# A Fourier mixing layer fused with an ELU feed-forward: a PSUM tile of its own for one product, two copies moved to another engine, a weight sum cut in pieces

## The chip, the cores and the metric

The kernel runs on one core of a Trainium2 chip. The core has TensorE (matmuls, called PE in the profile, its weight loads PEld), VectorE (DVE), ScalarE (ACT), GpSimd (POOL) and SyncE (SP), which work side by side and wait for each other by semaphores. TensorE writes its results into PSUM, which has eight banks of 2 KB per partition; VectorE and ScalarE read them from there, and POOL works here on SBUF alone. The metric is the device time of one execution in microseconds, lower is better; the time before is the median of three runs.

## The reference

The input x has 8 batches of 3008 rows and 256 columns. Cut to what matters:

```python
X = np.fft.rfft(x, axis=1)
Xr, Xi = X.real, X.imag
Yr = Xr @ w_r - Xi @ w_i + b_r
Yi = Xr @ w_i + Xi @ w_r + b_i
Yr = sign(Yr) * maximum(abs(Yr) - 0.01, 0)          # the same for Yi
y = np.fft.irfft(Yr + 1j * Yi, n=3008, axis=1)      # 24064 x 256 over all batches
h = y @ w_in                                        # w_in 256 x 2048
g = where(h > 0, h, exp(minimum(h, 0)) - 1)         # ELU
out = g @ w_out                                     # w_out 2048 x 256, float32
```

## The kernel before

Each batch goes through a Fourier part in small units, and then through the feed-forward. The feed-forward sets the rhythm: it is one long run of 376 steps, 47 for each batch. Step i computes two 128-row slices of h for 512 rows of y (`front`, line 966: four bf16 matmuls of 512 columns, L986), the ELU of them (`elu` and `finish_elu`), and two steps later the part of the output that they give (`back`, line 1044: eight float32r matmuls of 256 columns, L1060). Every eighth step ends a block of 512 rows, and its output is copied from PSUM into `osb` (L1072), half by VectorE and half by ScalarE.

The units of the Fourier part of the next batch are put into the steps, at most one per step, by `plan` (line 1090): X (second stage of the forward transform, 8 units), M (the complex product with w_r and w_i, 12 units), B and Y (the inverse transform, 6 and 8 units) and A (first stage of the forward transform for the batch after, 6 units). In a middle batch the order is y2, y3, X0 to X7, M(0,0), M(0,1), y4, M(1,0), M(1,1), y5, B0, M(2,0), M(2,1), y6, B1, M(3,0), M(3,1), y7, B2, M(4,0), M(4,1), B3, M(5,0), M(5,1), A0, B4, B5, A1 and so on; the steps after that hold no unit.

The order of all instructions is that of the program (`manual_schedule`): each engine takes its own in the order in which they are written. In one step that is: the unit (its matmuls, and the copy of its result out of PSUM), the step's front matmuls, ScalarE's part of the ELU, then `finish_elu`, VectorE's last part of the ELU **of the step before** (gT, L1028 or L1030), then what stands in the list f1 (loads, other side work), then `elu`, and `back` of two steps ago.

The ELU has two forms that matter here. In a "pool" step ScalarE makes two exponentials of 512 columns (L1002), POOL takes the minimum with 1 (L1039), and VectorE makes gT in two pieces. In an "act" step ScalarE makes a relu and an exponential of 1024 columns (L1004, L1005), POOL has no part, and VectorE makes gT in one piece of 1024. Steps with an M unit are act steps, and so are those listed in `on_act` (line 1115): X4, X7, B3, A0 and y4 to y7. In those listed steps the unit's result is copied by VectorE; in the other X, Y, B and A units of a middle batch it is copied by ScalarE.

PSUM is shared out so: two banks for the output (`psO`), two slots of two banks for h (`psH`), and one slot of two banks (`psF`) for the units; in some free steps h goes there too (`third`). With two slots for h, the front matmuls of step i wait until VectorE has made gT of step i - 2. Every unit that takes the psF slot waits until the unit before it has been copied out.

From batch 2 on, M forms the complex product out of three real ones (`unit_M`, line 246). The sums Xr + Xi are made ahead by POOL (`sum_XT`, L206), and wcat_s is changed once into the differences of weights that this needs (`three_weights`, line 214, L218, two POOL operations). M's six matmuls (L269) write one psF tile: first the shared product, of the sum and w_r, into the second bank; then the other two products into the first. In the first unit, M(0,0), the shared product comes last, because its sum is the last to be ready. VectorE copies the shared product to SBUF (the copy of 256 columns, called from L275, at L126) and adds it to the other two (L276); POOL adds the bias and makes the soft threshold (L281 to L283), in three operations per M.

Copies out of PSUM go through the helper `evac`, so that they all stand at L126 (VectorE) or L128 (ScalarE); what is copied is told by the names of the tiles (XT<-xps for X, yT<-yps for Y, yb<-mps for M).

Of the kernel before, what the change touches and what calls it, by code (L numbers as in the profile page):

```python
# [11 lines left out]
F32 = mybir.dt.float32  # L12
# [17 lines left out]
def kernel(  # L30
# [12 lines left out]
    P = nc.NUM_PARTITIONS  # L43

    B, S, D = x.shape
# [15 lines left out]
    wcat_r = constp.tile([P, 2, 2 * D], BF16, name="wcat_r")  # L61
    wcat_s = constp.tile([P, 2, 2 * D], BF16, name="wcat_s")
# [14 lines left out]
    space = constp.tile([P, 384], BF16, name="space")  # L77
# [41 lines left out]
    def unit_ps(name, alone):  # L119
        if alone:  # L120
            return pre2.tile([P, 2, 512], F32, name=name, tag="pre2")
        return psF.tile([P, 2, 512], F32, name=name, tag="fps")

    def evac(dst, src, on_dve):
        if on_dve:
            nc.vector.tensor_copy(dst, src)  # L126
        else:
            nc.scalar.copy(dst, src)  # L128
# [82 lines left out]

        return XS[:, 3 * dt + ch] if 3 * dt + ch < 5 else busy[:]

    def three_weights(c):

        v, r = (w[:, :, D * c : D * c + D] for w in (wcat_s, wcat_r))
        a, b_ = (r, v) if c else (v, r)
        nc.gpsimd.tensor_tensor(v, a, b_, ALU.subtract)  # L218

# [26 lines left out]
    def unit_M(b, q, i):  # L246
        if b == 1:
            if i == 0:
                mps_of[q] = unit_ps("mps", False)
            yb, clip = m_group(b, q, i, mps_of[q][:, i, :])  # L250
            nc.gpsimd.tensor_scalar(clip[:], yb, LAM, -LAM, ALU.min, ALU.max)
            nc.gpsimd.tensor_tensor(Y_of[b, q][:, i, :], yb, clip[:], ALU.subtract)
            return
        XT, o = XT_of[b], (2 * q + i) * P
        if i == 0:
            Y_of[b, q] = wk3.tile([P, 2, 2 * D], BF16, name="Y", tag="Y")
        ps = unit_ps("mps", False)
        ch, oc = divmod(o, 512)
        r, s = wcat_r, wcat_s
        todo = [  # L260
            (ps[:, 1, 0:D], None, r[:, :, 0:D]),
            (ps[:, 0, 0:D], XT[:, :, 1, o : o + P], s[:, :, 0:D]),
            (ps[:, 0, D : 2 * D], XT[:, :, 0, o : o + P], s[:, :, D : 2 * D]),
        ]
        if o == 0:
            todo.append(todo.pop(0))
        for out_, lhs, w in todo:
            for dt in range(2):
                nc.tensor.matmul(  # L269
                    out_, lhsT=lhs[:, dt] if lhs is not None else sum_of(dt, ch)[:, oc : oc + P],  # L270
                    rhs=w[:, dt, :], start=(dt == 0), stop=(dt == 1),
                )
        yb = wk3.tile([P, 2 * D], F32, name="yb", tag="yb")
        clip = wk2.tile([P, 2 * D], F32, name="clip", tag="clip")
        evac(yb[:, D : 2 * D], ps[:, 1, 0:D], True)  # L275
        nc.vector.tensor_tensor(  # L276
            yb[:].rearrange("p (c d) -> p c d", c=2),
            ps[:, 0].rearrange("p (c d) -> p c d", c=2),
            yb[:, D : 2 * D].unsqueeze(1).to_broadcast([P, 2, D]), ALU.add,
        )  # L280
        nc.gpsimd.tensor_tensor(yb[:], yb[:], bias_bc[:], ALU.add)  # L281
        nc.gpsimd.tensor_scalar(clip[:], yb[:], LAM, -LAM, ALU.min, ALU.max)  # L282
        nc.gpsimd.tensor_tensor(Y_of[b, q][:, i, :], yb[:], clip[:], ALU.subtract)  # L283
# [682 lines left out]
    def front(i, third, on_act, halves):  # L966
        blk, fp = divmod(i, NPAIR)
        early = i < FILL
        if early:
            hps = two_banks((psS0, psS1)[i % 2], "sps")  # L970
        elif third:
            hps = psF.tile([P, 2, TB], F32, name="hps", tag="fps")
        else:
            hps = psH.tile([P, 2, TB], F32, name="hps", tag="hps")
        todo = []
        for s in range(2):
            ft = 2 * fp + s
            for piece in sorted(pieces(blk * TB, TB), key=lambda z: z[3] - z[2]):
                todo.append((s, ft, piece))
        if i == PER // NPAIR * NPAIR:  # L980
            todo.sort(key=lambda z: z[2][0])
        Et = late3.tile([P, 2, TB], F32, name="Et", tag="Et")
        E_ = Et[:]
        for s, ft, (b, t0, c0, c1) in todo:
            for dt in range(2):
                nc.tensor.matmul(  # L986
                    hps[s][:, c0:c1] if early else hps[:, s, c0:c1],
                    lhsT=w_in_s[:, dt, ft * P : ft * P + P],
                    rhs=yT_of[b][:, dt, t0 : t0 + c1 - c0],
                    start=(dt == 0), stop=(dt == 1),  # L990
                )
            if early and (dt, c1) == (1, TB):
                nc.scalar.activation(E_[:, s], hps[s][:], AF.Exp)
        if early:
            return hps, Et
        if i == n - 1:
            for h in range(2):
                t = slice(TB // 2 * h, TB // 2 * h + TB // 2)
                nc.scalar.activation(E_[:, :, t], hps[:, :, t], AF.Exp)
        elif halves:  # L1000
            for s in range(2):
                nc.scalar.activation(E_[:, s], hps[:, s], AF.Exp)  # L1002
        elif on_act:
            nc.scalar.activation(E_, hps[:], AF.Relu, scale=-1.0)  # L1004
            nc.scalar.activation(E_, E_, AF.Exp, scale=-1.0)  # L1005
        else:
            nc.scalar.activation(E_, hps[:], AF.Exp)
        return hps, Et
# [25 lines left out]
    def elu(i, hps, Et, on_pool, on_act):  # L1034

        E_ = Et[:]
        if on_pool:
            for s in parts(i):
                nc.gpsimd.tensor_scalar(E_[s], E_[s], 1.0, 0.0, ALU.min, ALU.max)  # L1039
        elif not on_act:  # L1040
            nc.vector.tensor_scalar(E_, E_, 1.0, -1.0, ALU.min, ALU.add)
        late_elu.append((i, hps, Et, on_pool or on_act, on_pool))
# [44 lines left out]
    def put(kind, b, *a):  # L1087
        return ({"A": unit_A, "X": unit_X, "M": unit_M, "B": unit_B, "Y": unit_Y}[kind], (b, *a))

    def plan(b):  # L1090
# [35 lines left out]
        for t, u in enumerate(seq, lead):  # L1126
            if b and n1 < B:
                mode[t] = "act" if u in on_act or u[0] == "M" else "pool"
            if mode[t] == "act" and u[0] != "M":
                k = {"y": "Y"}.get(u[0], u[0])  # L1130
                c = {"y": b, "A": n2}.get(u[0], n1)
                if c < B:
                    f0[t].append(put(k, c, u[1], False, *((False, True) if k == "B" else (True,))))
            elif u[0] == "y":
                f0[t].append(put("Y", b, u[1]))
            elif u[0] == "n":
                f0[t].append(put("Y", n1, u[1]))
            elif u[0] == "A":
                if n2 < B:
                    f0[t].append(put("A", n2, u[1]))  # L1140
            else:
                f0[t].append(put(u[0], n1, *u[1:]))
            if u == (("A", 1) if b and n2 < B else ("B", 5)):
                f1[t] += [
                    (load_Bs, (n1, w, 0, 4 * K1 - 16 * (b == w == 0))) for w in range(4)
                ]
            if u == ("A", 5) and n2 < B:
                f1[t] += [(load_Z, (n2, s0, s1)) for s0, s1 in ((0, 8), (8, NS))]
# [12 lines left out]
        if n2 < B:  # L1161
            for ci in range(3):
                f1[xs[ci]].append((load_x, (n2, ci)))
        if b == 1:
            for c in range(2):
                f1[2 * c].append((three_weights, (c,)))
        if b and n1 < B:
            for dt, t in ((0, 6), (1, 9)):
                f0[t].append((sum_XT, (n1, dt)))
# [5 lines left out]
    for i in range(n + LAG):  # L1175
        if i == FILL:
            few.close()
            psH, psF = (
                ctx.enter_context(
                    tc.tile_pool(  # L1180
                        name=n_, bufs=k_, space=bass.MemoryType.PSUM, reuse_waits="tile"
                    )
                )
                for n_, k_ in (("psH", 2), ("psF", 1))
            )
        if i == LAG:
            back(0, False)
# [21 lines left out]
        if i < n:  # L1209
            for f, a in f1[r]:  # L1210
                f(*a)
            split = i > LAG and (i - LAG) % NPAIR == NPAIR - 1
            if split:
                back(i - LAG, True)
            elu(i, *h, pooled, on_act)
            if 1 <= i < 5:
                if i < 3:
                    scale_w_in(2, True, i - 1)
                scale_w_in(3, False, (i - 1) // 2, (i - 1) % 2)
            if i == n - 2:  # L1220
                early_h = front(n - 1, True, False, True)
            elif early_h:
                early_h = None
        else:
            split = False
# [32 lines left out]
```

## Time and profile before

| | |
|---|---|
| median of 3 runs | 906.11 us (904.94 to 3122.65) |
| the profiled execution | 905.32 us, span 903.5 us |
| granted TensorE clock in it | 0.998 |
| DVE copy yb<-mps, 128x256 (L126) | 72 times, 424 ns |
| DVE sum yb<-mps,yb, 128x512 (L276) | 72 times, 691 ns |
| POOL L281, L282, L283 | 72 times each, 1280, 614 and 1284 ns |
| XT<-xps, 128x768, by ACT / by DVE | 47 times 798 ns / 13 times 958 ns |
| POOL sum of weights (L218) | 2 times, at 162.1 and 166.4 us, about 1165 ns |

One execution was recorded by the profiler; its span is the time between the first and the last instruction. A line of a timeline gives start and duration in microseconds, the engine, the line of the kernel, the operation, what it writes and reads, and, in square brackets, how long the engine had been idle just before and which engine's work ended that. A line of the list of waits reads: engine, what and line, "<-" what it waited for, then the total in microseconds, how often, and the longest. Matmuls overlap, and the end of a matmul is modelled, so a busy TensorE isn't always one at its peak; the distances between starts of matmuls are the better measure.

### The profile page before, as it was taken

The numbers are of one execution on the slowest core, as the hardware profiler recorded it, in microseconds if no ns is written. First come the engines' busy times: TensorE is split into PE (matmuls) and PEld (weight loads), VectorE is DVE, ScalarE is ACT, GpSimd is POOL, SyncE is SP. The second block draws the span as 40 slices with busy tenths as digits, with TensorE's granted clock in tenths as the row PEclk, the third lists the DMA queues.
The fourth block names the chain that finished last, engine by engine and source line by source line (L and its number), as shares of the span: only waits on it lengthen the run. The fifth ranks groups of instructions, "written<-read, shape, count | busy, mean of one in ns | idle before, by whom it ended". The sixth has DMA issues, their size and how long they took to land.

```text
span 903.5 us, 18114 instructions
## 1 busy us (share of the span) xinstructions
PE 877.8 (97%) x6814; PEld 668.5 (74%) x6917; DVE 689.9 (76%) x978; ACT 716.4 (79%) x991; POOL 595.0 (66%) x802
## 2 busy tenths in 40 slices
PE   8999999999999999999999999999999999999997
PEld 3467667777787777877779777787777877777776
DVE  8788768688866887678867888668786688778776
ACT  6778788888878889788887888878887888877664
POOL 7561550787667875688856877569775687753664
PEclk9999999999999999999999999999999999999999
DMA  8996226531373215532264232732328011231011
GB/s 262 310 259 187 85 69 189 149 118 48 115 212 115 74 56 156 164 117 77 77 198 114 98 103 59 216 115 78 104 77 233 26 42 53 70 95 48 24 48 47
DMA packets 90494, 105.85 MB, mean 117 GB/s; under 512 B 5363, under 2 KB 81142, under 8 KB 86982
## 3 DMA queue, kind: packets, MB, share of 16 engines
q1 hardware_dynamic: 84054, 76.64, 30.5%
q0 software_dynamic: 5968, 27.26, 9.5%
q8 instruction: 54, 0.88, 0.4%
q10 hardware_dynamic: 384, 0.79, 0.3%
q14 instruction: 34, 0.28, 0.1%
HBM read 54.86 MB, written 49.81 MB: 116 GB/s over the span
## 4 chain that ended last, share of the span: by engine, by line
PE 79%; DVE 11%; DMA 3%; issue 3%; ACT 2%; POOL 1%; DVEq 0%; SPq 0%; ACTq 0%; POOLq 0%
PE ps_o L1060 32%; PE hps L986 31%; DVE gT L1028 6%; PE mps L269 4%; PE bps L355 2%; PE xps L189 2%; DVE yb L276 2%; DMA Z<-DA 2%; DVE yb L126 2%; PE aps L152 2%; PE mps L229 2%; PE yps L518 1%; PE sps L986 1%; DMA xt<-in_x_dram 1%; POOL yb L281 1%
## 5 line engine op out<-in xcount | busy, mean ns | idle before, releaser
L1028 DVE SCALAR_TENSOR_TENSOR gT<-Et,hps 128x512 fp32r<-128x512 f32 (+1 forms) x544 | 424.6, 812 | 144.3 <-POOL Et L1039 110.5
L1060 PE MATMUL ps_o<-w_out_r,gT 128*128 128x256 f32 x3008 | 476.2, 301 | 0.0
L1060 PEld LDWEIGHTS ps_o<-w_out_r,gT 128*128 128x128 f32 x3008 | 403.7, 189 | 48.6 <-DVE osb L1072 1.3
L1039 POOL TENSOR_SCALAR Et<-Et 128x512 f32<-128x512 f32 x432 | 257.1, 613 | 219.3 <-ACT Et L1002 209.2
L986 PE MATMUL hps<-yT,w_in_s 128*128 128x512 bf16 (+6 forms) x1593 | 370.7, 350 | 12.2 <-DVE gT L1028 5.4
L1002 ACT ACTIVATE Et<-hps 128x512 f32<-128x512 f32 x410 | 223.4, 600 | 64.1 <-PE hps L986 58.3
L986 PEld LDWEIGHTS <-w_in_s 128*128 128x128 bf16 x1728 | 142.8, 98 | 125.9 <-issue 30.3
L1004 ACT ACTIVATE Et<-hps 128x1024 f32<-128x1024 f32 x132 | 135.6, 1027 | 70.0 <-PE hps L986 69.5
L1005 ACT ACTIVATE Et<-Et 128x1024 f32<-128x1024 f32 x132 | 139.6, 1057 | 4.2
L281 POOL TENSOR_TENSOR yb<-yb,bias_bc 128x512 f32<-128x512 f32 x72 | 92.1, 1280 | 16.5 <-DVE yb L276 16.4
L283 POOL TENSOR_TENSOR Y<-yb,clip 128x512 bf16<-128x512 f32 x72 | 92.4, 1284 | 6.0
L276 DVE TENSOR_TENSOR yb<-mps,yb 128x512 f32<-128x512 f32 x72 | 49.8, 691 | 2.5
L126 DVE COPY yb<-mps 128x256 f32<-128x256 f32 x72 | 30.5, 424 | 25.7 <-PE mps L269 20.5
L282 POOL TENSOR_SCALAR clip<-yb 128x512 f32<-128x512 f32 x72 | 44.2, 614 | 6.3
L128 ACT CAST A<-aps 128x1024 bf16<-128x1024 f32 x37 | 37.6, 1015 | 12.3 <-PE aps L152 11.1
L128 ACT CAST XT<-xps 128x768 bf16<-128x768 f32 x47 | 37.4, 798 | 9.0 <-PE xps L189 8.8
L269 PE MATMUL mps<-wcat_s,XT 128*128 128x256 bf16 x288 | 43.3, 273 | 0.0
L128 ACT CAST Bz<-bps 128x1024 bf16<-128x1024 f32 x36 | 36.1, 1002 | 0.4 <-PE bps L355 0.4
L1030 DVE SCALAR_TENSOR_TENSOR gT<-hps,Et 128x1024 fp32r<-128x1024 f32 x28 | 34.2, 1223 | 2.3
L206 POOL TENSOR_TENSOR XS<-XT 128x512 bf16<-128x512 bf16 x30 | 34.1, 1161 | 2.2 <-DVE XT L126 2.2
L189 PE MATMUL xps<-M,Z 96*128 96x96 bf16 x480 | 30.9, 207 | 1.8 <-DMA Z<-DA 1.3
L1072 DVE COPY osb<-ps_o 128x512 f32<-128x512 f32 x46 | 31.5, 686 | 0.3
(184 smaller groups left out, 680.9 us busy)
## 6 DMA issues: line engine op xcount, KB each, us to landing
xt<-in_x_dram POOLq DMA_DIRECT2D x21, 1024.0 KB, 5.5
out_dram<-osb SPq DMA_DIRECT2D x158, 128.0 KB
Bs<-DB SPq DMA_DIRECT2D x30, 384.0 KB
DB<-Bz SPq DMA_DIRECT2D x20, 512.0 KB
DA<-A SPq DMA_DIRECT2D x19, 512.0 KB
Z<-DA SPq DMA_DIRECT2D x6, 1152.0 KB
xt<-in_x_dram POOLq DMA_DIRECT2D x6, 512.0 KB, 6.0
Z<-DA SPq DMA_DIRECT2D x8, 384.0 KB
```

The lines of the kernel that those rows point to most:

```text
L128: nc.scalar.copy(dst, src)
L269: nc.tensor.matmul(out_, lhsT=lhs[:, dt] if lhs is not None else sum_of(dt, ch)[:, oc : oc + P], rhs=w[:, dt, :], start=(dt == 0), stop=(d ...
L276: nc.vector.tensor_tensor(yb[:].rearrange("p (c d) -> p c d", c=2), ps[:, 0].rearrange("p (c d) -> p c d", c=2), yb[:, D : 2 * D].unsqueez ...
L281: nc.gpsimd.tensor_tensor(yb[:], yb[:], bias_bc[:], ALU.add)
L283: nc.gpsimd.tensor_tensor(Y_of[b, q][:, i, :], yb[:], clip[:], ALU.subtract)
L986: nc.tensor.matmul(hps[s][:, c0:c1] if early else hps[:, s, c0:c1], lhsT=w_in_s[:, dt, ft * P : ft * P + P], rhs=yT_of[b][:, dt, t0 : t0 + ...
L1002: nc.scalar.activation(E_[:, s], hps[:, s], AF.Exp)
L1004: nc.scalar.activation(E_, hps[:], AF.Relu, scale=-1.0)
L1005: nc.scalar.activation(E_, E_, AF.Exp, scale=-1.0)
L1028: nc.vector.scalar_tensor_tensor(o, e, -1.0, h, ALU.add, ALU.max)
L1039: nc.gpsimd.tensor_scalar(E_[s], E_[s], 1.0, 0.0, ALU.min, ALU.max)
L1060: nc.tensor.matmul(po[q][:, i_ % 2, :], lhsT=gT[:, s, i_ * P : i_ * P + P], rhs=w_out_r[:, ft, :], start=(ft == 0 and i_ % 2 == 0), stop=( ...
```

## The change

The change has three parts.

- `unit_M` from batch 2 on takes two PSUM tiles of one bank each in place of one tile of two banks: `k1` for the shared product, `ps` for the other two. They come from a pool `psM` that takes turns with `psF` on the same two banks: the new function `last_banks` closes the one that is open and opens the other, when another one is asked for. The order of the matmuls is kept. The copy of the shared product reads `k1`, so it depends on that tile's two matmuls; the sum reads `ps` and the copy.
- X4 and X7 stay act steps, but their copy out of PSUM goes to ScalarE: the last argument of `put` becomes `k != "X"`.
- `three_weights` takes a half of the rows at a time, so that two POOL operations of 512 elements per partition become four of 256. They stood in f1 of the first and third step of batch 1's period, ahead of `elu`; now one each follows `elu` in its first four steps.

```diff
@@ unit_ps
-        return psF.tile([P, 2, 512], F32, name=name, tag="fps")
+        return last_banks("psF").tile([P, 2, 512], F32, name=name, tag="fps")
+
+    open_pool = {}
+
+    def last_banks(name):
+
+        if name not in open_pool:
+            for _, stack in open_pool.values():
+                stack.close()
+            open_pool.clear()
+            stack = ctx.enter_context(ExitStack())
+            pool = stack.enter_context(
+                tc.tile_pool(
+                    name=name, bufs=1 if name == "psF" else 2,
+                    space=bass.MemoryType.PSUM, reuse_waits="tile",
+                )
+            )
+            open_pool[name] = pool, stack
+        return open_pool[name][0]
@@ three_weights
-    def three_weights(c):
-
-        v, r = (w[:, :, D * c : D * c + D] for w in (wcat_s, wcat_r))
+    def three_weights(c, dt):
+
+        v, r = (w[:, dt, D * c : D * c + D] for w in (wcat_s, wcat_r))
@@ unit_M
-        ps = unit_ps("mps", False)
+        ps, k1 = (
+            last_banks("psM").tile([P, 2 * D], F32, name="mps", tag="mps") for _ in range(2)
+        )
...
-            (ps[:, 1, 0:D], None, r[:, :, 0:D]),
-            (ps[:, 0, 0:D], XT[:, :, 1, o : o + P], s[:, :, 0:D]),
-            (ps[:, 0, D : 2 * D], XT[:, :, 0, o : o + P], s[:, :, D : 2 * D]),
+            (k1[:, 0:D], None, r[:, :, 0:D]),
+            (ps[:, 0:D], XT[:, :, 1, o : o + P], s[:, :, 0:D]),
+            (ps[:, D : 2 * D], XT[:, :, 0, o : o + P], s[:, :, D : 2 * D]),
...
-        evac(yb[:, D : 2 * D], ps[:, 1, 0:D], True)
+        evac(yb[:, D : 2 * D], k1[:, 0:D], True)
...
-            ps[:, 0].rearrange("p (c d) -> p c d", c=2),
+            ps[:].rearrange("p (c d) -> p c d", c=2),
@@ front
-            hps = psF.tile([P, 2, TB], F32, name="hps", tag="fps")
+            hps = last_banks("psF").tile([P, 2, TB], F32, name="hps", tag="fps")
@@ plan
-                    f0[t].append(put(k, c, u[1], False, *((False, True) if k == "B" else (True,))))
+                    f0[t].append(
+                        put(k, c, u[1], False, *((False, True) if k == "B" else (k != "X",)))
+                    )
...
-        if b == 1:
-            for c in range(2):
-                f1[2 * c].append((three_weights, (c,)))
@@ the loop over the steps
-            psH, psF = (
-                ctx.enter_context(
-                    tc.tile_pool(
-                        name=n_, bufs=k_, space=bass.MemoryType.PSUM, reuse_waits="tile"
-                    )
+            psH = ctx.enter_context(
+                tc.tile_pool(
+                    name="psH", bufs=2, space=bass.MemoryType.PSUM, reuse_waits="tile"
                 )
-                for n_, k_ in (("psH", 2), ("psF", 1))
             )
...
             elu(i, *h, pooled, on_act)
+            if PER <= i < PER + 4:
+                three_weights(*divmod(i - PER, 2))
```

## The prediction

> **What bounds the kernel now.** I read the busy times first, then the chain that ended last, then the waits, then the timeline of one batch.
>
> ```profile
> PE 877.8 (97%) x6814; PEld 668.5 (74%) x6917; DVE 689.9 (76%) x978; ACT 716.4 (79%) x991; POOL 595.0 (66%) x802
> ...
> PE 79%; DVE 11%; DMA 3%; issue 3%; ACT 2%; POOL 1%; DVEq 0%; SPq 0%; ACTq 0%; POOLq 0%
> ```
>
> TensorE sets the pace; the rest of the chain is mostly VectorE. Only what removes a hole on TensorE is worth time. The list of waits says where VectorE gets late:
>
> ```profile
> ACT Et L1004 <- PE hps L986: 69.5, 119, 1.2
> ...
> PEld L986 <- issue: 30.3, 120, 0.6
> DVE yb L126 <- PE mps L269: 20.5, 37, 1.1
> ...
> PE hps L986 <- DVE gT L1028: 5.4, 19, 0.6
> ```
>
> The copy of the shared product (L126) waits 20.5 us for TensorE in 37 of its 72 runs, and TensorE's front matmuls (L986) in turn wait for VectorE's gT (L1028), which frees their PSUM slot. The timeline around units M(1,0), M(1,1) and y5 (some lines left out) shows how one makes the other:
>
> ```profile
> 515.84 0.39 PE L269 MATMUL mps<-wcat_r,XS 128*128 128x256 bf16 x2
> ...
> 516.07 0.60 PE L269 MATMUL mps<-wcat_s,XT 128*128 128x256 bf16 x4
> ...
> 516.70 0.42 DVE L126 COPY yb<-mps 128x256 f32<-128x256 f32 x1 [0.72 <-PE mps L269]
> ...
> 517.16 0.69 DVE L276 TENSOR_TENSOR yb<-mps,yb 128x512 f32<-128x512 f32 x1
> ...
> 517.77 1.21 DVE L1028 SCALAR_TENSOR_TENSOR gT<-Et,hps 128x1024 fp32r<-128x1024 f32 x1
> ...
> 518.90 0.68 DVE L1072 COPY osb<-ps_o 128x512 f32<-128x512 f32 x1
> 519.03 1.02 PE L986 MATMUL hps<-yT,w_in_s 128*128 128x512 bf16 x4
> 519.50 0.41 DVE L126 COPY yb<-mps 128x256 f32<-128x256 f32 x1
> ...
> 521.82 1.02 PE L986 MATMUL hps<-yT,w_in_s 128*128 128x512 bf16 x4 [0.48 <-DVE gT L1028]
> ```
>
> The shared product is finished at 516.23 (515.84 + 0.39), but its copy starts at 516.70, just after the sixth matmul's end at 516.67, with VectorE idle for 0.72. Copy, sum and gT run in a row to 518.98, and the front matmuls start at 519.03.
>
> How much TensorE loses this way comes from the matmuls' start times. After the last matmul of a unit the first front matmul starts, when nothing holds it, 0.109 us later (M), 0.041 (y), 0.201 (B) or 0.238 (A): the least that each shows. What is over that, summed from 184 to 778 us over all six batches: **4.3 us after M, 8.15 after y, 1.45 after A0, 0.8 after B, and 0.8 once at 776.7**, 15.5 us in all (0.25 after each X5 is apart, below). In 4.3 of the 15.5, VectorE has an extra copy just ahead (osb, L1072, 0.69; Bz or A, 1.22); 11.2 are without one.
>
> **The change, part by part.** *The copy at the shared product's end.* Nothing is added: two one-bank tiles in place of one of two banks, the same six matmuls, copy (0.425) and sum (0.691). The copy may start four matmuls earlier, 4 x 0.109 = **0.44 us**, where VectorE stands idle; the sum then needs copy and last matmul, which end together (second matmul's end + 0.42 against + 0.44). So gT, and the slot it frees, come up to 0.44 earlier. From an M's first matmul at T, undisturbed: copy T+0.42, sum T+0.88, gT done T+2.79. The next M's front is due at T+2.45+0.67 = T+3.12: its hole goes. A y's front is due at T+2.78: its hole falls to some 0.05. ScalarE doesn't take over as the limit: relu (1.03), exp (1.06), gT (1.21) and the front (1.02) with 0.15 of gaps give 4.47 from a front's start to the next but one, and M, M, y need 4.56 from the first M's front to y's (5.23 - 0.67).
>
> Worked through for the batch at 508 to 564 us, each time shifted by what has been won before: y4 starts 0.31 earlier (0.11 of it is ready sums, below), y5 0.26 more, y6 0.36 more, y7 0.17 more. In M(1,1) VectorE is held by the osb copy, not by TensorE (no idle before the copy at 519.50), and y5 keeps most of its 0.645. The last M units and A0 follow a Bz cast of 1.22 on VectorE, and bring 0.2 to 0.3 each. In the first unit of a batch, M(0,0), the shared product comes last and nothing is won.
> Scaled to all batches: holes without an extra copy, 11.2 us, of which 1.7 (A0, and the one at 776.7) half, 0.9, and of the other 9.5 us 85%, 8.0 (y4 keeps 0.13); those with one, 4.3 us, a third (y5 and y7 won 0.43 of the 1.48 us in and before them), 1.4. **Together 10.3 us**; between 0 and 15.5 as the ends.
>
> *X4 and X7 on ScalarE.* Twelve casts of 0.958 leave VectorE, twelve of 0.798 (the rows of XT by engine) come to ScalarE, ahead of that step's relu.
>
> ```profile
> 499.92 0.96 DVE L126 CAST XT<-xps 128x768 bf16<-128x768 f32 x1
> ...
> 500.79 1.03 ACT L1004 ACTIVATE Et<-hps 128x1024 f32<-128x1024 f32 x1 [0.58 <-PE hps L986]
> ...
> 506.64 0.96 DVE L126 CAST XT<-xps 128x768 bf16<-128x768 f32 x1 [0.54 <-PE xps L189]
> ...
> 507.50 1.02 ACT L1004 ACTIVATE Et<-hps 128x1024 f32<-128x1024 f32 x1 [1.06 <-PE hps L986]
> ```
>
> ScalarE is idle for 1.06 us ahead of X7's relu, waiting for the front matmuls; 0.80 fits in. At X4 it fits too, but for this batch, where an osb copy leaves 0.58 and the relu comes 0.2 later. VectorE's relief lets gT of X3 and X6 go earlier. The hole of 0.256 before the front of X5, the same in all six batches, closes, but X6's front then waits for gT of X4, whose relu, exp and gT are unmoved (end 504.15, front now 504.29): 0.09 is left of it. 5 x 0.09 less 0.13 in this batch: **0.3 us**. X7's copy ends 0.1 earlier, POOL's sums for M(0,0) with it (counted in y4). Without ScalarE's cover the twelve casts cost 12 x 0.80 = 9.6 us.
> Here a rule of the Trainium skill speaks against the change: "ScalarE: Activation LUTs", section "Rules for kernel authors", gives plain arithmetic to VectorE, as up to about three times as fast per element there in bf16. By it the casts would grow on the move and outlast the cover, and the sum below would fall by up to the 9.6. The XT rows, 958 on VectorE and 798 on ScalarE from PSUM, say the reverse, so the sum keeps them.
>
> *Sums of weights.* Two POOL operations (1.16 each, at 162.1 and 166.4), ahead of POOL's minimum, become four of half the size behind it: each between half a row of 1.16 (0.58) and a whole one. I take 0.6. No hole on TensorE lies in this stretch but one for Z's DMA, and POOL idles about 0.98 per pool-mode step until ScalarE's exp; that hides them, and nothing is won. At 1.16 each, minimum and sum need 2.35 of a 2.18 step: 4 x 0.17 = 0.7 us at worst if nothing took it up.
>
> *The switch of pools.* It issues no instruction. The units that follow M waited for M's sum on VectorE before and wait for copy and sum now, the copy being first. New is that an M's shared product and its other two products wait for different things.
>
> **Sum**: 10.3 + 0.3 = 10.6 off the profiled execution's own 905.3 (span 903.5): 894.7. The median shown is 906.11, 0.8 above it: **895.5 us**, 1.2% faster. No change can be told from one of 2% here.
>
> **Rivals.** *Nothing won* (0.10): the copy goes early, but the time is given back behind it (VectorE's load over M, M, y, M, M, y is 4 x 2.33, copy, sum and gT, + 2 x 2.15, cast and gT, + some 0.5 of osb = 14.1 us against TensorE's 4 x 2.45 + 2 x 2.18 = 14.2, so VectorE has no room of its own), or the copy still waits for all six matmuls. For it: the holes with an osb copy. Against: 0.55 us idle on average before 37 copies. 904 to 906.
> *ScalarE becomes the bound at X4 and X7* (0.08): ScalarE is late when X4 starts, the cover is gone and each cast goes into the chain relu, exp, gT, front: 9.6 us against the 10.3. It begins to cost from a lateness of 1.06 - 0.80 = 0.26. Against: 0.2 us idle per step in X0 to X3. 905. The skill's rule above belongs beside this one.
> *The second wait inside M breaks TensorE's stream* (0.07; slower): the four matmuls behind the shared product now carry a wait of their own, and each costs what a weight load held at a wait costs, 30.3 / 120 = 0.25 us. 72 x 0.25 = 18 us, less 10.6: 913. It decides from 10.6 / 72 = 0.15 per M. Against: a front matmul whose slot is free follows M's last matmul by 0.109, the ordinary distance, though it waits too.
>
> **Chances.** Forecast (890 to 900.5) 0.72, its ends 40% and all of the holes; the rivals 0.10, 0.08, 0.07; more than all holes 0.03. The range takes in the forecast and the first two rivals: 889.5 to 906.5. Faster by over 2% (below 888) 0.04, slower by over 2% (above 924) 0.03, within 0.93.
>
> **What would show it.** The copy starts within 0.05 of the second matmul's end wherever VectorE is free, and its wait for TensorE falls from 20.5 us to some 5; the holes after M nearly vanish, those after y fall from 8.15 to about 2.5, the rest being those with an osb copy; XT's casts number 59 on ScalarE and 1 on VectorE, and the relu at X7 starts where it did; the hole before X5 moves to X6; L218 has four rows of 0.6 to 1.2 with no hole near them. The forecast is wrong if distances above 0.11 appear between M's second and third matmul, if ScalarE's relu at X4 starts over 0.3 late, or if VectorE's gT now waits for exp where it waited for nothing.

## The result and the profile after

The changed kernel takes 896.16 us (median of six runs) against 904.53 us of the kernel before; the ratio, worked out from the single runs, is 0.9904, with a 95% interval of 0.9885 to 0.9924 (the quotient of the two medians is 0.9907). One of the six runs before took 3122.65 us and has no part in the ratio. That is 1% faster, and within the 2% that count as a difference here. The profiled execution took 895.53 us with a span of 893.8, against 905.32 and 903.5 before.

Busy times and chain of the changed kernel, from the page of its profile:

```profile
PE 873.2 (98%) x6814; PEld 669.1 (75%) x6917; DVE 677.7 (76%) x966; ACT 725.1 (81%) x1003; POOL 594.7 (67%) x804
...
PE 83%; DVE 6%; ACT 4%; DMA 3%; issue 2%; POOL 2%; DVEq 0%; SPq 0%; ACTq 0%; POOLq 0%
```

TensorE does the same work in a shorter span. VectorE's share of the chain that ended last has gone from 11% to 6%; ScalarE's from 2% to 4%. The list of waits of the changed kernel (L144, L289, L296, L1006, L1024 and L1025, L1048, L1080 and L1092 are the L126, L269, L276, L986, L1004 and L1005, L1028, L1060 and L1072 of before):

```profile
ACT Et L1024 <- PE hps L1006: 44.8, 83, 1.2
DVE gT L1048 <- ACT Et L1025: 35.9, 35, 1.7
...
PEld L1006 <- issue: 22.1, 90, 0.7
DVE yb L144 <- PE mps L289: 13.1, 28, 1.1
...
PE hps L1006 <- DVE gT L1048: 1.8, 6, 0.5
...
PEld ps_o L1080 <- ACT osb L1092: 1.1, 5, 0.3
```

The copy's wait for TensorE fell from 20.5 us to 13.1, TensorE's direct wait for gT from 5.4 to 1.8, and the idle time ahead of the front matmuls' weight loads, which the profile puts down to no other engine ("issue"), is 22.1 us in place of 30.3. The last line has no counterpart before; it comes back below. The timeline of the same units as before, M(1,0), M(1,1) and y5:

```profile
510.77 0.39 PE L289 MATMUL mps<-wcat_r,XS 128*128 128x256 bf16 x2
...
510.99 0.60 PE L289 MATMUL mps<-wcat_s,XT 128*128 128x256 bf16 x4
...
511.19 0.42 DVE L144 COPY yb<-mps 128x256 f32<-128x256 f32 x1
...
511.72 0.69 DVE L296 TENSOR_TENSOR yb<-mps,yb 128x512 f32<-128x512 f32 x1
...
512.33 1.21 DVE L1048 SCALAR_TENSOR_TENSOR gT<-Et,hps 128x1024 fp32r<-128x1024 f32 x1
...
513.46 0.68 DVE L1092 COPY osb<-ps_o 128x512 f32<-128x512 f32 x1
...
513.91 1.03 PE L1006 MATMUL hps<-yT,w_in_s 128*128 128x512 bf16 x4
514.06 0.41 DVE L144 COPY yb<-mps 128x256 f32<-128x256 f32 x1
...
516.45 1.02 PE L1006 MATMUL hps<-yT,w_in_s 128*128 128x512 bf16 x4 [0.21 <-DVE gT L1048]
```

The shared product ends at 511.16 and its copy starts at 511.19, while the other four matmuls run to 511.59. gT is done at 513.54, and the next front matmuls start at 513.91 without a hole. Then the osb copy stands ahead of M(1,1)'s copy, and the front of y5 is still held, by 0.38 us in place of 0.65.

**How the two traces are compared.** The way from the span's start to the tenth step alone differs by up to 1.9 us from one profiled execution to another, the same code in it, so spans are a poor measure of single microseconds. I use the stretch from the back matmuls of step 55 to those of step 330 (185.4 to 816.9 us before), and sum in it the distances between the starts of neighbouring matmuls, by what stands on either side. The change against before, in us:

| kernel | stretch | front after M | after y | after A0 | after X | inside M | inside back |
|---|---|---|---|---|---|---|---|
| changed | -9.5 | -3.0 | -5.3 | -1.1 | -0.5 | -0.55 | **+1.4** |
| copy alone | -8.4 | -3.05 | -5.0 | -1.1 | 0 | 0 | +1.2 |
| casts alone | -0.85 | 0 | -0.1 | 0 | -0.4 | -0.5 | +0.2 |
| weights alone | -0.1 | 0 | 0 | 0 | 0 | 0 | 0 |
| shared product last | -1.0 | 0 | -0.15 | 0 | -0.5 | -0.5 | +0.15 |
| shared product second | -5.3 | -2.4 | -1.5 | -0.4 | -0.4 | -0.5 | +0.5 |
| without VectorE's osb | -11.75 | -3.8 | -6.8 | -1.45 | -0.4 | -0.5 | +1.6 |
| exponential behind osb | -10.15 | -2.8 | -5.3 | -1.1 | -0.2 | -0.5 | -0.5 |

(A 0 stands for less than 0.1. What a row leaves out is up to 0.35 in one place, and 0.8 more in front matmuls after B in the last row.) The prediction's holes, counted as there, are 15.5 us before and 5.5 after: after M 4.3 and 1.3, after y 8.15 and 2.7, after A0 1.45 and 0.4, after B 0.8 and 0.6, and the one behind the last M unit 0.8 and 0.45.

### The profile page after: what moved, and what is told of

It reads as the page before. It is cut to its first block, busy times and chain, and to the rows that moved or that the text cites. A ratio compares the mean times of both kernels' runs of the same rounds, so it can differ in the third digit from the quotient of the medians.

```text
span 893.8 us, 18170 instructions
## 1 busy us (share of the span) xinstructions
PE 873.2 (98%) x6814; PEld 669.1 (75%) x6917; DVE 677.7 (76%) x966; ACT 725.1 (81%) x1003; POOL 594.7 (67%) x804
## 4 chain that ended last, share of the span: by engine, by line
PE 83%; DVE 6%; ACT 4%; DMA 3%; issue 2%; POOL 2%; DVEq 0%; SPq 0%; ACTq 0%; POOLq 0%
PE ps_o L1080 35%; PE hps L1006 32%; PE mps L289 4%; DVE gT L1048 3%; PE xps L207 2%; PE bps L375 2%; PE aps L170 2%; PE yps L538 2%; PE ips L553 1%; PE mps L247 1%; DMA Z<-DA 1%; ACT Et L1024 1%; DMA w_in_f<-in_moe_w_in_dram 1%; DMA xt<-in_x_dram 1%; ACT Bz L146 1%
## 5 line engine op out<-in xcount | busy, mean ns | idle before, releaser
L1048 DVE SCALAR_TENSOR_TENSOR gT<-Et,hps 128x512 fp32r<-128x512 f32 (+1 forms) x544 | 424.5, 812 | 154.6 <-POOL Et L1059 118.4
L1080 PE MATMUL ps_o<-w_out_r,gT 128*128 128x256 f32 x3008 | 477.6, 301 | 0.2
L1080 PEld LDWEIGHTS ps_o<-w_out_r,gT 128*128 128x128 f32 x3008 | 404.1, 189 | 49.6 <-DVE osb L1092 1.3
L1006 PE MATMUL hps<-yT,w_in_s 128*128 128x512 bf16 (+6 forms) x1593 | 370.9, 350 | 7.3 <-DVE gT L1048 1.8
L1006 PEld LDWEIGHTS <-w_in_s 128*128 128x128 bf16 x1728 | 142.2, 98 | 116.2 <-issue 22.1
L1024 ACT ACTIVATE Et<-hps 128x1024 f32<-128x1024 f32 x132 | 135.6, 1027 | 49.6 <-PE hps L1006 44.8
L1025 ACT ACTIVATE Et<-Et 128x1024 f32<-128x1024 f32 x132 | 139.6, 1057 | 4.2
L146 ACT CAST XT<-xps 128x768 bf16<-128x768 f32 x59 | 47.1, 800 | 10.3 <-PE xps L207 10.1
L296 DVE TENSOR_TENSOR yb<-mps,yb 128x512 f32<-128x512 f32 x72 | 49.8, 692 | 7.4 <-DVE yb L144 0.5
L289 PE MATMUL mps<-wcat_s,XT 128*128 128x256 bf16 x288 | 43.3, 273 | 0.0
L144 DVE COPY yb<-mps 128x256 f32<-128x256 f32 x72 | 30.4, 422 | 14.0 <-PE mps L289 13.1
L1092 DVE COPY osb<-ps_o 128x512 f32<-128x512 f32 x46 | 31.5, 685 | 0.3
```

The lines of the kernel that those rows point to most:

```text
L289: nc.tensor.matmul(out_, lhsT=lhs[:, dt] if lhs is not None else sum_of(dt, ch)[:, oc : oc + P], rhs=w[:, dt, :], start=(dt == 0), stop=(d ...
L296: nc.vector.tensor_tensor(yb[:].rearrange("p (c d) -> p c d", c=2), ps[:].rearrange("p (c d) -> p c d", c=2), yb[:, D : 2 * D].unsqueeze(1 ...
L1006: nc.tensor.matmul(hps[s][:, c0:c1] if early else hps[:, s, c0:c1], lhsT=w_in_s[:, dt, ft * P : ft * P + P], rhs=yT_of[b][:, dt, t0 : t0 + ...
L1048: nc.vector.scalar_tensor_tensor(o, e, -1.0, h, ALU.add, ALU.max)
L1080: nc.tensor.matmul(po[q][:, i_ % 2, :], lhsT=gT[:, s, i_ * P : i_ * P + P], rhs=w_out_r[:, ft, :], start=(ft == 0 and i_ % 2 == 0), stop=( ...
```

## The experiments

### The early copy alone

The kernel before with `ps` and `k1` as tiles of their own and `last_banks`, and nothing else of the change:

```diff
-        ps = unit_ps("mps", False)
+        ps, k1 = (
+            last_banks("psM").tile([P, 2 * D], F32, name="mps", tag="mps") for _ in range(2)
+        )
```

> The kernel before with one part of the change: the shared product in a PSUM tile of its own. X4 and X7 are still copied by VectorE, the sums of weights are whole and ahead of the minimum. Theory (the early copy makes the gain): holes before the front matmuls after M, y, B, A0 and at the end of the last batch fall by 9 us or more of 15.5, time 0.8 to 1.1% under the kernel before; the hole of 0.256 before the front of X5 stays. Rival (VectorE's relief of twelve casts is what makes room for it): under half of the gain, above 900 us.

Measured: 896.23 us against 903.98, ratio 0.9922 (0.9908 to 0.9937). The holes fall from 15.5 to 5.8 us, by 9.7; the hole before X5 stays at 0.256 in all six batches. The early copy needs no help from the casts: 8.4 of the 9.5 us in the stretch are its own.

### The two casts alone

```diff
-                    f0[t].append(put(k, c, u[1], False, *((False, True) if k == "B" else (True,))))
+                        put(k, c, u[1], False, *((False, True) if k == "B" else (k != "X",)))
```

> The kernel before with X4 and X7 copied by ScalarE, nothing else. Theory: worth 0.3 to 1 us: the hole of 0.256 before the front of X5 closes in all six batches and one of 0.15 to 0.2 opens before X6; the relu at X7 starts where it did; the holes after M and y lose at most 0.1 each for the ready sums of M(0,0). Rival (VectorE's relief carries the gain): 4 us or more. Rival (ScalarE becomes the bound): 5 us or more slower.

Measured: 903.19 us against 903.98, ratio 0.9994 (0.9984 to 1.0003): not to be told from nothing by time. The trace says 0.85 us. The hole before X5 is gone, and in five of six batches one of 0.20 to 0.22 stands before X6. The timeline of this kernel around X5 and X6, some lines left out:

```profile
500.24 1.22 DVE L1028 SCALAR_TENSOR_TENSOR gT<-Et,hps 128x1024 fp32r<-128x1024 f32 x1 [1.71 <-ACT Et L1005]
...
500.95 0.51 PE L189 MATMUL xps<-M,Z 96*128 96x96 bf16 x8
...
501.52 1.02 PE L986 MATMUL hps<-yT,w_in_s 128*128 128x512 bf16 x4
...
503.88 0.80 ACT L128 CAST XT<-xps 128x768 bf16<-128x768 f32 x1 [0.22 <-PE xps L189]
...
504.75 1.03 ACT L1004 ACTIVATE Et<-hps 128x1024 f32<-128x1024 f32 x1
```

gT of X4 has waited 1.71 us for the exponential, ends at 501.46, and X6's front follows at 501.52. What VectorE was relieved of is idle time now: the chain through relu and exponential sets X6's front. At X7 the cast on ScalarE ends at 504.68 and the relu follows at 504.75, right behind the front's matmuls (503.68 + 1.03), so the cover holds.

### The sums of weights alone

```diff
-        if b == 1:
-            for c in range(2):
-                f1[2 * c].append((three_weights, (c,)))
...
             elu(i, *h, pooled, on_act)
+            if PER <= i < PER + 4:
+                three_weights(*divmod(i - PER, 2))
```

> The kernel before with the sums of weights in four pieces behind the minimum, nothing else. Theory: nothing, within 0.3 us in the holes before the front matmuls; each piece 0.6 to 0.7 us. A rival by which the late minimum in two steps held TensorE gives 1 to 2 us.

Measured: 904.27 us against 903.98, ratio 1.0005 (0.9996 to 1.0015); the holes are 15.4 us against 15.5. This part is worth nothing that can be seen.

### The shared product last

The changed kernel, with the order of the three products turned round in every M:

```diff
-        if o == 0:
-            todo.append(todo.pop(0))
+        todo.append(todo.pop(0))
```

> The changed kernel, but in every M the shared product comes last of the three, as it does in M(0,0). It still has a tile of its own, and the pools still take turns. Theory (the gain is the lead of 0.44 us of the copy): the copy waits for the sixth matmul again, its wait for TensorE is back at 17 to 21 us, the holes after M and y are back within 1.5 us of those before, time within 0.3% of the kernel before. Rival (the gain comes from two tiles that come free one by one): most of the gain stays, under 899 us. Rival (the wait in the midst of M, or the turn-taking of pools, has a cost that the gain covers): slower than the kernel before by 0.5% or more.

Measured: 902.58 us against 903.98, ratio 0.9989 (0.9980 to 0.9999), and holes of 15.4 us. The wait of the copy in this kernel's list of waits:

```profile
DVE yb L144 <- PE mps L288: 24.4, 38, 1.2
```

Two tiles, turn-taking pools and casts are all there, and the kernel is back where it was, but for the 1.0 us in the stretch that the casts bring. So the gain is the lead of the copy, not the way in which the banks come free, and neither the turn-taking nor the second wait inside M costs anything that shows. The wait came out above the 17 to 21 expected, because VectorE, rid of X7's cast, now stands idle for longer ahead of M(0,0)'s copy.

### The shared product second

The changed kernel with the shared product between the other two, so that half of the lead is left:

```diff
-        if o == 0:
-            todo.append(todo.pop(0))
+        todo.insert(2 if o == 0 else 1, todo.pop(0))
```

> The changed kernel, but the shared product comes second of the three, so that two matmuls follow it in place of four and the copy leads by 0.22 us in place of 0.44 (M(0,0) as it is). Theory (each hole shrinks by the lead until it is gone): the holes after M, mostly under 0.22, go as with the whole lead, to 1.2 to 1.8 us; those after y, mostly 0.17 to 0.44, lose some 0.2 each and keep 3.5 to 5 us; time 0.6 to 0.75% under the kernel before. Rival (gain in proportion to the lead): half the holes' gain, after M about 2.8, after y about 5.5, time 0.4 to 0.5% under.

Measured: 898.50 us against 904.05, ratio 0.9941 (0.9924 to 0.9958); holes 10.7 us, after M 1.9, after y 6.6. The time, 0.59% under the kernel before with an interval of 0.42 to 0.76%, doesn't part the two expectations (0.6 to 0.75% and 0.4 to 0.5%); the holes have to. Neither expectation holds for the parts. The holes after M go almost as with the whole lead, but those after y lose only 1.5 us, far less than 0.2 each. Together they lose 4.8 of the 10.0 us that the whole lead takes, just under a half, so in the sum the rival is right: gain in proportion to the lead. My theory took the hole of the second M and that of the following y for two holes that each shrink by the lead. They are one lateness of VectorE: what closes the first lets TensorE come earlier to the second, and the lead is spent. The traces bear this out row by row. In the 18 rows of M, M and y in which both Ms have the lead, the three holes together were 0.37 to 0.76 us before; half the lead, 0.22 us, takes 0.09 to 0.22 off each row, and never twice the 0.22.

### Without VectorE's osb copy

```diff
+            if split and q == 0:
+                copy(osb[:, 0:2, 0:8], po[q][:, :, 0:8])
-            if not (last and q):
+            elif not (last and q):
...
-                            ov[w, r0 : r0 + k // 8], osb[c0 : c0 + k, i_, :]
+                            ov[w, r0 : r0 + k // 8],
+                            bias_bc[c0 : c0 + k, 0:E] if split and q == 0 else osb[c0 : c0 + k, i_, :],
```

> The changed kernel with VectorE's half of the osb copy cut to 16 elements per partition (about 0.15 us in place of 0.69); the output rows of that half are stored from the bias instead, so a part of the output is left out. Theory (what is left of the holes after M and y are the steps where VectorE copies osb ahead of M's copy): the holes after y fall from 2.7 to 1.3 us or less, those after M, A0 and at the end of the last batch from 2.2 to 1.3 or less, 2 to 3 us together. Rival (they are what ScalarE's relu and exp leave): the holes stay within 0.7 us.

Measured: 891.43 us against 904.05, ratio 0.9857 (0.9842 to 0.9871). The cut copy takes 0.169 us in place of 0.685. The holes fall from 5.5 to 2.9 us: after y from 2.7 to 1.3, those after M, A0 and behind the last M unit from 2.2 to 1.0. The holes of 0.39 after M(5,1) and 0.37 after A0 vanish, those of 0.38 and 0.44 at y5 and y7 too, and the one of 0.71 at 189.9 us goes to 0.21. So of the 4.9 us that the change leaves in these places, 2.6, about half, are the steps in which VectorE copies osb ahead of M's copy; what holds TensorE for the rest was not followed.

### ScalarE's osb copy ahead of the exponential

Where a block of output ends in an act step, ScalarE's half of osb comes between relu and exponential:

```diff
-            nc.scalar.activation(E_, E_, AF.Exp, scale=-1.0)
+            late_exp.append(lambda: nc.scalar.activation(E_, E_, AF.Exp, scale=-1.0))
+            if not (i > LAG and (i - LAG) % NPAIR == NPAIR - 1):
+                late_exp.pop()()
...
                 back(i - LAG, True)
+            while late_exp:
+                late_exp.pop()()
```

This asks where the 1.4 us inside the back matmuls come from, which the changed kernel loses more than the kernel before. Its timeline shows one of them, at the first back matmuls of a new block:

```profile
642.58 1.06 ACT L1025 ACTIVATE Et<-Et 128x1024 f32<-128x1024 f32 x1
...
643.29 1.60 PE L1080 MATMUL ps_o<-w_out_r,gT 128*128 128x256 f32 x8
643.54 0.57 ACT L1092 COPY osb<-ps_o 128x512 f32<-128x512 f32 x1
...
644.16 0.54 PEld L1080 LDWEIGHTS ps_o<-w_out_r,gT 128*128 128x128 f32 x4 [0.25 <-ACT osb L1092]
```

TensorE is half through its eight matmuls when it needs the output bank that ScalarE copies out, and ScalarE came to that copy only behind its exponential.

> The changed kernel; in act steps in which a block of output ends, ScalarE makes its half of the osb copy between relu and exponential in place of behind both. Nothing else moves. Theory (in the changed kernel TensorE comes earlier to the next block's matmuls, and waits there for ScalarE's osb copy, 1.2 to 1.4 us in all that the kernel before did not lose): the distances inside the back matmuls fall by 1 us or more, the wait of weight loads for ScalarE's osb copy goes; the exponential is 0.57 later in these steps, which may open holes after y of up to 0.3 each; between 1 us faster and 1 us slower than the changed kernel. Rival (the longer distances in the back matmuls come from weights or clock): they stay.

Measured: 893.69 us against 904.05, ratio 0.9883 (0.9868 to 0.9898). All of these distances are gone (no back matmul in the units' part comes over 0.04 us late, where 13 did in the changed kernel and seven, less late, before), 1.9 us less inside the back matmuls than in the changed kernel. Of that 0.9 us is lost again before the front of B units and 0.2 before that of X units; the stretch is 0.7 us shorter than the changed kernel's. Ahead of B, TensorE now waits for the gT of the M two units earlier. In the case at 643.6 us that gT starts at 642.37, right behind y's cast on VectorE (641.41 + 0.93) and the exponential, now later (641.27 + 1.06), which end together.

### The changed kernel and the last one side by side

> The changed kernel itself, to stand beside the next one on the same chip: 0.85 to 1.1% under the kernel before.

> The changed kernel with ScalarE's half of osb between relu and exponential, once more. By the distances of its matmuls it is 0.5 to 0.9 us shorter than the changed kernel in the stretch of the units (1.9 us gone inside the back matmuls, 0.9 lost before the front of B and some at X5): 0.05 to 0.1%, too little to be told apart by times. Rival (the 2.5 us between the two medians so far are its own): 0.25% or more under the changed kernel.

Measured on one chip against 904.74: the changed kernel 894.77 us, ratio 0.9892 (0.9874 to 0.9910); with the exponential behind osb 894.07 us, ratio 0.9880 (0.9863 to 0.9897). In the stretch they are 9.3 and 10.25 us shorter than before. The second is the shorter in both pairs of traces, by 0.7 and 0.9 us; the times alone can't part the two.

## Why the prediction was right

**The mechanism.** TensorE sets the pace, and what it lost in the M units came from VectorE's row of copy, sum and gT behind the sixth matmul. The copy now starts 0.037 to 0.039 us after the shared product's end in 12 of the 22 cases in which VectorE was idle for it by more than 0.12 us (0.105 to 0.107 in the other ten, below), and turning the order round takes the whole gain back.

**The copy's term, 10.3 us.** The holes that it is about fell by 10.0. Its two parts, parted in the traces by whether an osb, Bz or A copy stands in VectorE's row just ahead, came out close as well: about 9 us from the holes without such a copy (8.9 said) and about 1 from those with one (1.4 said). Two of the latter grew, from 0.63 to 0.71 before a y4 and from 0.31 to 0.39 after an M(5,1). In the batch that was worked through by hand, the front of y4 keeps 0.11 (0.13 was left to it), y5 0.38 and y7 0.44 of 0.65 and 0.63. This batch is 1.8 us shorter from step 188 to 235 against 1.5 from its shifts. After y 2.7 us are left (2.5 said), after M 1.3 (said to nearly vanish: osb again).

**The casts, 0.3 us and 0.1 per batch for the ready sums.** The trace of the casts alone has 0.85 us: 0.44 at the front of X units, with the hole moved to X6 as said, 0.54 inside M(0,0) and 0.1 after y, less 0.2 inside the back matmuls. ScalarE's cover held, and the rival by which it becomes the bound has nothing for it. The rule of the Trainium skill ("ScalarE: Activation LUTs", "Rules for kernel authors") gives its figure for bf16 operations with one source, while these casts read 32-bit values out of PSUM, so the two don't speak of the same case. For these casts the rows decide: the 59 on ScalarE take 800 ns in the mean after the change, against 958 on VectorE before.

**The sums of weights, nothing**: nothing.

**The size of the whole.** 10.6 us were predicted off the profiled execution; the profiled executions differ by 9.8, the medians by 8.4 in the first comparison and 10.0 in the second. That the forecast of 895.5 us lies so near to the measured 896.16 is in part luck: it started 1.6 us too high, from the 906.11 of three runs where six give 904.53, and took off 2.2 us too much. The step that failed is the equation of holes closed with time won. Holes and the distances inside M gave 11.0 us in the stretch, and 1.4 came back inside the back matmuls: TensorE, earlier at the start of a new block, meets ScalarE's osb copy, which stands behind the exponential. I had named what waits for VectorE behind each M and not what else waits at a place that TensorE would now reach earlier. That this is the cause was shown by moving the exponential.

**The rivals.** The second wait inside M: in 37 of the 72 Ms the third matmul does carry a wait of its own in the changed kernel, and it follows the second by 0.109 us in the median and 0.110 at most; the distances between the second and the sixth matmul are 0.109 each in the median in both kernels, and a whole M, from its first matmul to its last, takes 0.556 us on average against 0.565. "Nothing won" fell with the copy alone. Nor does VectorE's gT wait for the exponential more than it did: 35.9 us in 35 cases, in the list above, against this line of the list before:

```profile
DVE gT L1028 <- ACT Et L1005: 33.6, 36, 1.4
```

**What was to show it** failed in two places. The copy was to start within 0.05 us of the shared product's end wherever VectorE is free, and in ten of the 22 cases it takes 0.105 to 0.107. And the copy's wait for TensorE fell to 13.1 us and not to 5. In M(0,0), where the shared product comes last, VectorE's idle time ahead of the copy grew from 2.6 to 6.3 us over the six batches, because X7's cast no longer fills it. One of these cases in the changed kernel:

```profile
504.38 0.42 DVE L144 COPY yb<-mps 128x256 f32<-128x256 f32 x1 [1.15 <-PE mps L289]
```

With the copy alone, where X7's cast still stands ahead, the wait is 9.4 us:

```profile
DVE yb L144 <- PE mps L289: 9.4, 28, 0.7
```

So the cast explains 3.7 of the 8.1 us by which the forecast of this wait was out. Most of the rest stands ahead of M(2,0), M(3,0) and M(4,0), each behind a B unit: VectorE was idle there for 13.4 us before and is for 5.6 now. Eighteen leads of 0.44 make 7.9, so the lead was won there, and what is left is the time in which TensorE has not yet come to the shared product's end. It costs nothing there, and the sum of a wait says little where the engine had nothing else to do.

## What to carry to other kernels

Where two results of one engine are read one after the other by the next, give the first a tile of its own, so that its reader waits for its own matmuls; the gain is about the lead, or less, for each lateness that it shortens, and two holes in a row that come from one lateness count once. Sum the holes of the engine that sets the pace by what stands on either side of them, rather than the waits of the others: that list also shows what is given back somewhere else. Before calling a hole won, look for the next thing that this engine will reach earlier, here a bank that another engine still holds.

## What the runs showed that was not expected

A copy of the shared product that waits for TensorE alone starts 0.036 to 0.039 us after the modelled end of the matmul. Where it has a second wait, for POOL, the wait for TensorE stands in a semaphore instruction of its own ahead of the copy, and the copy starts 0.105 to 0.107 us after the matmul's end; so it is in the kernel before (35 and 15 cases) and in the changed one (12 and 10). The second wait makes the copy about 0.07 us later here.

Half of a POOL sum doesn't take half of its time. Two rows of the changed kernel's groups:

```profile
L236 POOL TENSOR_TENSOR wcat_s<-wcat_s,wcat_r 128x256 bf16<-128x256 bf16 x2 | 1.4, 677 | 0.0
L236 POOL TENSOR_TENSOR wcat_s<-wcat_r,wcat_s 128x256 bf16<-128x256 bf16 x2 | 1.3, 668 | 0.0
```

Against 1161 and 1169 ns for twice the elements, this makes a fixed part of about 0.18 us for each operation (2 x 0.672 less 1.165), an estimate that takes the rest to go with the number of elements.

The opening of the kernel, the same code in all of them, took between 76.4 and 78.3 us to its tenth step in the profiled executions. What is left open is where in the opening this comes from; it was not followed.
